# Block attention and gated MLP on one core: the order of all instructions set by a list scheduler in the kernel

## The chip, the core and the metric

One core of a Trainium2 chip. It has five engines that run at the same time, each in the order of its own queue: TensorE (matmul, PE in the rows; its weight loads are PEld), VectorE (DVE), ScalarE (ACT), GpSimd (POOL) and SyncE (SP), which here only starts DMA transfers. They wait for each other through semaphores. The metric is the device time of the one core in microseconds (us), the median of several runs.

## The reference

Eight images (batch) of 576 tokens with 8 heads of 64. Attention works only inside chunks of 64 tokens; its output, laid side by side over the heads, is the input of a gated MLP whose gate mixes tokens:

```python
scores = scale * np.matmul(q_c, k_c.transpose(0, 1, 2, 4, 3))     # 64x64 blocks
attn = np.exp(scores - max); attn = attn / (sum + 1e-09)
x = np.matmul(attn, v_c)                                           # (8, 576, 512)
h = gelu_tanh(x @ w_in)                                            # 512 -> 1024
u, v = h[..., :512], h[..., 512:]
v_n = (v - mu) / np.sqrt(var + 1e-06) * g_ln
v_s = np.einsum('ts,bsd->btd', w_sg, v_n) + b_sg[None, :, None]
out = x + (u * v_s) @ w_out
```

## The kernel before

All is float32, and each big product is done as three products of a high and a low part (names ending in h and l). The tokens are cut into 36 tiles of 128 for the attention; a tile passes through `att_scores` (S: matmuls of line 380 or 411, then maximum, exponential and sum on VectorE and ScalarE, then the division), `att_transpose` (T: VectorE's 32x32 transpose of line 450 and copies of lines 453 to 460 on ScalarE and VectorE, which write `ptT`; the first five tiles are transposed on TensorE, line 441), and `att_out` (O: matmuls of line 478 or 498, then `keep` splits the result into `xh` and `xl`).

For each image there are then `v_unit` (five or four token tiles, 12 matmuls each, line 544; gelu into `hs`, statistics of lines 550 to 553, scaling of lines 559 to 568 into `v` or `z`), four `u_unit` (24 matmuls, line 581, gelu into `u2`), four `s_unit` (the token mixing, 28 matmuls, line 601; `gh` and `gl` are the split gate), and the output product: `o_unit` for images 0 and 1, `o_fast` for the others (seven block products, line 672). `w_sums` makes sums of blocks of `w_out` on GpSimd for `o_fast` (tiles `r`, tag `tmp`, lines 250 to 274), once, in image 2. The weights `w_in` come as 64-bit words and are split in `pair_begin` and `pair_end` (L, W, w for the v half, X, x for the u half), `w_out` in `o_w` (Y). `keep_clock` (D) runs matmuls on a constant whose result nobody reads.

The string `START` (line 44) is the order in which the code of images 0 and 1 calls these steps; the loop at line 771 does the rest, with the attention of the next image put into slots between the units by `SLOTS`. The tile layer below takes the code's order as a priority, keeps a model of its own, and orders every engine's queue from that. Buffers come from pools: the tag `tmp` has four (`hs`, `blocks`, `ot`, `r`, staging), PSUM `pm` has four, `u2`, `v`, `pt` and `ptT` one each.

Of the kernel before, what the change touches and what calls it, by code (L numbers as in the profile page):

```python
# [3 lines left out]

# [5 lines left out]

F32 = mybir.dt.float32
F32R = mybir.dt.float32r
# [65 lines left out]
G_BLOCK = {(0, 0): 0, (1, 0): 1, (1, 1): 2, (0, 1): 3}  # L78


def segments(t):
# [9 lines left out]

@with_exitstack
def block_attention_gated_mlp(ctx: ExitStack, tc: tile.TileContext, qkv, w_in, w_out, w_sg, g_ln, b_sg, out):
    nc = tc.nc
    const = ctx.enter_context(tc.tile_pool(name="const", bufs=1))
    att = ctx.enter_context(tc.tile_pool(name="att", bufs=2))
    xp = ctx.enter_context(tc.tile_pool(name="xp", bufs=2))
    mp = ctx.enter_context(tc.tile_pool(name="mp", bufs=1))
    tmp = ctx.enter_context(tc.tile_pool(name="tmp", bufs=4))
    small = ctx.enter_context(tc.tile_pool(name="small", bufs=3))  # L100
    ps_m = ctx.enter_context(tc.tile_pool(name="ps_m", bufs=4, space=PSUM))

    def split(hi, lo, src, hi_eng, lo_eng):
        if hi_eng is nc.scalar:
# [466 lines left out]

    u2 = {}

    def u_unit(b, dt):
        pm = ps_m.tile([P, 2, 512], F32, name="pm")
        dc = slice(dt * P, (dt + 1) * P)
        i = 0
        for kt in range(KT):
            for a, c in ((win_l, xh[b]), (win_h, xl[b]), (win_h, xh[b])):
                for j in range(2):  # L580
                    nc.tensor.matmul(  # L581
                        pm[:, j, :HS], a[:, kt, dc], c[:, kt, j * HS : (j + 1) * HS], start=(i == 0), stop=(i == 11)
                    )
                i += 1
        if dt == 0:
# [155 lines left out]
    def att_slots(b, n):  # L741
# [18 lines left out]
    def keep_clock(n):  # L760

        spare = ps_m.tile([P, 2, 512], F32, name="pm")
        for _ in range(n):
            nc.tensor.matmul(spare[:, 0, :P], ident, ident, start=True, stop=True)

    steps["D"] = keep_clock
    steps["G"], steps["g"] = lambda k: load_w_sg(), split_w_sg
    steps["Y"] = lambda k: o_w(k // 2, k % 2)
# [2 lines left out]
    for b in range(2, B):  # L771
# [3 lines left out]
        slots = att_slots(b, len(units))  # L775
        for i, ((f, k), after) in enumerate(zip(units, slots)):
# [5 lines left out]
            for g, tiles in after:  # L782
                g(*tiles)
    o_fast(B - 1, 3)


# [42 lines left out]
```

## Time and profile before

| | |
|---|---|
| median of 3 runs | 534.28 us (534.09 to 535.17) |
| the profiled execution | 533.52 us, of which the span of the trace is 531.7 |
| instructions in the trace | 12411 |
| mean granted clock of TensorE | 0.981 of 2.4 GHz |
| DMA | 46.58 MB, mean 88 GB/s |
| ScalarE table loads | 32, mean 1283 ns |

The page gives one execution. TensorE is the busiest engine, and what it waits for is the first thing to read; a stretch in which its clock is low costs time without any wait being shown. The engines that feed it (VectorE and ScalarE for the attention tiles) are read by what stands in their queues before the instruction that TensorE waits for.

### The profile page before, as it was taken

What the parts mean: (1) busy time and instruction counts of PE and PEld (TensorE: products, weight loads), DVE (VectorE), ACT (ScalarE), POOL (GpSimd) and SP (SyncE); (2) the same over time, 40 slices, a digit from 0 to 9 for tenths busy, and PEclk for the clock granted to TensorE, in tenths of its full rate; (3) what the DMA queues carried; (4) which work ended last, traced back from release to release, by engine and by line L of the source; (5) the groups of instructions that cost most, each with busy time, mean ns of one, the idle gap of its engine ahead of it and who ended that gap; (6) DMA issues with size and microseconds to landing.
All of it is one profiled execution on the core that took longest, in us unless ns stands there. A gap on an engine that the chain in (4) does not pass through costs nothing.

```text
span 531.7 us, 12411 instructions
## 1 busy us (share of the span) xinstructions
PE 499.4 (94%) x5202; PEld 460.9 (87%) x5206; DVE 381.2 (72%) x719; ACT 287.9 (54%) x493; POOL 85.1 (16%) x83
## 2 busy tenths in 40 slices
PE   1999998899999979999999989999999979999996
PEld 1776888799999869998999879988999869998996
DVE  6895849986766787797658685797758685476156
ACT  5679557762433868537752477427752577313221
POOL 0032300030110257011300131011300131002000
PEclk9999998999999979999999999999999998999999
DMA  8765011212245522415120422414121400010002
GB/s 331 286 191 176 0 41 44 80 46 75 95 165 131 168 60 61 121 35 138 48 71 30 152 48 82 120 46 138 42 68 40 150 21 20 2 66 24 1 1 89
DMA packets 52683, 46.58 MB, mean 88 GB/s; under 512 B 35218, under 2 KB 45458, under 8 KB 52628
## 3 DMA queue, kind: packets, MB, share of 16 engines
q1 hardware_dynamic: 52628, 45.80, 27.8%
q8 instruction: 41, 0.67, 0.5%
q14 instruction: 14, 0.11, 0.1%
HBM read 36.34 MB, written 9.44 MB: 86 GB/s over the span
## 4 chain that ended last, share of the span: by engine, by line
PE 44%; DVE 10%; ACT 6%; POOL 2%; issue 1%; DVEq 0%; POOLq 0%; ACTq 0%
PE pm L601 12%; PE pm L581 11%; PE pm L672 11%; PE pm L544 7%; PE pm L478 2%; DVE gl L108 1%; POOL sm L553 1%; DVE sm L550 1%; DVE pt L387 1%; DVE nmax L384 1%; DVE v L562 1%; DVE xl L523 1%; ACT L391 1%; ACT xh L520 1%; DVE u L626 1%
## 5 line engine op out<-in xcount | busy, mean ns | idle before, releaser
L601 PE MATMUL pm<-wsg,v 128*128 128x288 f32 x768 | 109.5, 299 | 0.0
L601 PEld LDWEIGHTS pm<-wsg,v 128*128 128x128 f32 x768 | 105.4, 191 | 0.4
L553 POOL TENSOR_TENSOR sm<-sm,neg_half 128x1 f32<-128x1 f32 x36 | 36.5, 1015 | 235.2 <-DVE sm L552 235.2
L581 PE MATMUL pm<-xh,win_l 128*128 128x288 f32 x256 | 58.3, 310 | 0.3 <-ACT win_l L190 0.3
L581 PE MATMUL pm<-xh,win_h 128*128 128x288 f32 x256 | 56.5, 303 | 0.0
L581 PE MATMUL pm<-xl,win_h 128*128 128x288 f32 x256 | 56.5, 303 | 0.0
L544 PE MATMUL pm<-win_h,xl 128*128 128x512 f32 x128 | 51.5, 402 | 0.0
L105 ACT CAST gh<-u 128x576 fp32r<-128x576 f32 x32 | 21.5, 673 | 54.7 <-DVE u L605 43.7
L544 PE MATMUL pm<-win_l,xh 128*128 128x512 f32 x128 | 50.7, 396 | 0.0
L544 PE MATMUL pm<-win_h,xh 128*128 128x512 f32 x128 | 50.6, 395 | 0.0
L398 POOL TENSOR_TENSOR pt<-pt,nmax 128x512 f32<-128x512 f32 x27 | 28.7, 1082 | 133.0 <-DVE nmax L395 133.0
L605 DVE TENSOR_TENSOR u<-pm,u 128x576 f32<-128x576 f32 x32 | 23.9, 748 | 32.7 <-PE pm L601 32.5
L581 PEld LDWEIGHTS pm<-xh,win_l 128*128 128x128 f32 x256 | 43.1, 196 | 2.3 <-ACT win_l L190 0.7
L581 PEld LDWEIGHTS pm<-xl,win_h 128*128 128x128 f32 x256 | 42.7, 196 | 0.0
L581 PEld LDWEIGHTS pm<-xh,win_h 128*128 128x128 f32 x256 | 42.5, 195 | 0.0
L561 ACT ACTIVATE v<-hs,sm 128x512 fp32r<-128x512 f32 x32 | 23.1, 723 | 28.5 <-POOL sm L553 28.2
L550 DVE BATCH_NORM_STATS2 sm<-hs 128x6 f32<-128x512 f32 x36 | 24.4, 687 | 17.1 <-ACT hs L547 17.1
L478 PE MATMUL pm<-ptT,av 64*64 64x64 f32 x928 | 22.9, 232 | 11.1 <-ACT ptT L458 5.3
L478 PEld LDWEIGHTS pm<-ptT,av 64*64 64x64 f32 x928 | 18.9, 142 | 16.3 <-ACT ptT L458 9.0
L562 DVE SCALAR_TENSOR_TENSOR v<-hs,sm,v 128x512 fp32r<-128x512 f32 x32 | 24.1, 755 | 12.2 <-ACT v L561 11.8
L453 ACT COPY ptT<-blocks 128x512 f32<-128x512 f32 x31 | 19.0, 620 | 24.6 <-DVE blocks L450 17.2
L108 DVE TENSOR_TENSOR gl<-u,gh 128x576 fp32r<-128x576 f32 x32 | 25.0, 782 | 8.5 <-ACT gh L105 8.4
(163 smaller groups left out, 1062.6 us busy)
## 6 DMA issues: line engine op xcount, KB each, us to landing
qk<-qkv SPq DMA_DIRECT2D x31, 512.0 KB, 4.4
out_dram<-ot SPq DMA_DIRECT2D x31, 288.0 KB, 2.2
av<-qkv SPq DMA_DIRECT2D x116, 64.0 KB, 2.7
wsg<-w_in SPq DMA_DIRECT2D x4, 512.0 KB, 4.4
wout<-w_in SPq DMA_DIRECT2D x4, 512.0 KB, 7.8
st<-w_out SPq DMA_DIRECT2D x8, 256.0 KB, 3.1
qkv_w<-qkv SPq DMA_DIRECT2D x2, 768.0 KB, 10.6
stage<-w_sg SPq DMA_DIRECT2D x5, 288.0 KB, 4.2
```

The source lines that it names most:

```text
L108: lo_eng.tensor_tensor(lo, src, hi.bitcast(F32), op=ALU.subtract)
L398: eng.tensor_tensor(pt[:, i], pt[:, i], den[:, i].unsqueeze(2).broadcast_to([P, H, D]), op=ALU.mult)
L478: nc.tensor.matmul(pm[o, c, i, h // 2, :], vt[r, place, :], ptT[r, place].rearrange("p a s -> p (a s)"), start=True, stop=True,)
L544: nc.tensor.matmul(pv, a[:, kt, tok], c[:, kt, DH:], start=(i == 0), stop=(i == 11))
L550: nc.vector.bn_stats(st, h)
L553: nc.gpsimd.tensor_tensor(rs, rs, neg_half, op=ALU.pow)
L561: nc.scalar.mul(hi, h, rs)
L562: nc.vector.scalar_tensor_tensor(lo, h, rs, hi.bitcast(F32), op0=ALU.mult, op1=ALU.subtract)
L581: nc.tensor.matmul(pm[:, j, :HS], a[:, kt, dc], c[:, kt, j * HS : (j + 1) * HS], start=(i == 0), stop=(i == 11))
L601: nc.tensor.matmul(pm[:, j, :HS], a[:, dc], c[:, m, j * HS : (j + 1) * HS], start=(i == 0), stop=(i == len(ops) - 1))
L605: nc.vector.tensor_tensor(row, pm[:, :, :HS], row, op=ALU.mult)
L672: nc.tensor.matmul(pm[:, e, :HS], a[:, k, e * P : (e + 1) * P], c[:, k, :], start=(first and i == 0), stop=(i == len(ops) - 1), skip_group ...
```

## The change

Every call on an engine is only recorded (`Recorder`, `Plan.add`): its operands, the buffers it uses and, by the cells of memory that it reads and writes, which earlier calls it must follow. Each gets a price from its shape (`Op.price`). After the last call, `emit` runs a list scheduler three times (`run`): every engine takes, among the calls whose inputs are there, the one with the earliest due time among those that can start within 200 ns of the first; TensorE takes the one that can start first among its next 96 matmuls; a buffer of a pool can be taken when its last user is done. Due times (`due`) go back from TensorE's order of the run before. The calls are then issued in the order of their planned starts, with the tile layer told to keep that order. Which instructions there are, and how many on each engine, stays the same.

```diff
-v01 A8 B8 O4 x0 X1 v02 x1 X2 v03 X3 v04 u00 x2 g0 g1 u01 x3 g2 g3 u02 P5 g4 u03 T5 s00 T6 P7 s01 Q5 s02 T7 T8
+v01 A8 B8 O4 x0 X1 v02 x1 X2 v03 X3 v04 U0 x2 g0 g1 U1 x3 g2 g3 g4 F0 u02 F1 P5 u03 T5 s00 T6 P7 s01 Q5 s02 T7 T8
...
+AHEAD = 96
+WAIT = {"tensor": 100, "gpsimd": 120}
...
+        if self.engine == "sync":
+            size = self.ins[0].size() * 4
+            return (460 if self.ins[0].ap[-1][1] >= P else 640), 2000 + size / 400
+        if self.engine == "vector":
+            one = len(self.ins) == 1 and not psum and self.method in ("tensor_copy", "tensor_scalar")
+            return 75 + (0.53 if one else 1.04) * n, 80
+        if self.engine == "scalar":
+            return 100 + 0.82 * n + (100 if len(self.outs) > 1 else 0), 100
+        return (850 if "pow" in str(self.kwargs.get("op")) else 200 + 1.8 * n), 42
...
+        at = None
+        for _ in range(3):
+            at = self.run(users, after, at)
+        engines = {getattr(self.nc, e).engine for e in ENGINES}
+        with tc.manual_schedule(engines=engines):
+            for k in sorted(range(len(ops)), key=lambda k: (at[k], k)):
+                op = ops[k]
+                getattr(getattr(self.nc, op.engine), op.method)(*op.args, **op.kwargs)
...
+                    ks = [k for k in tensor[pe : pe + AHEAD] if start[k] is None]
...
+                t0 = min(found)[0]
+                if e == "tensor":
+                    t, k = min(found)
...
+                t, k = min(
+                    (late[k] + (1300 if ops[k].table not in (0, table) else 0), b, k) for b, k in found if b <= t0 + 200
+                )[1:]
...
-    nc = tc.nc
-    const = ctx.enter_context(tc.tile_pool(name="const", bufs=1))
...
+    nc = Plan(tc.nc)
...
-    make_identity(nc, eye)
+    nc.gpsimd.memset(eye, 0.0)
+    nc.gpsimd.affine_select(
+        out=eye, in_=eye, compare_op=ALU.not_equal, fill=1.0, base=0, pattern=[[-1, P]], channel_multiplier=1
+    )
...
+        if later:
+            held[dt] = pm
+        else:
+            u_act(dt, pm)
...
+    nc.emit(tc)
```

`U0` and `F0` part a `u_unit` of image 0 into its matmuls and its gelu. In the changed kernel every row carries line 224, since all calls are issued there; the names of the tiles tell them apart.

SyncE at the start of the program, before (`wsg`, `wout` receive the v half of `w_in`, `qk`, `qkv` and `av` the attention inputs of tiles 0 to 4):

```order
L214 DMA wsg_0_105<-w_in 128x1024
L346 DMA qk_107<-qkv 128x1024
L355 DMA av_109<-qkv 128x512
L346 DMA qk_111<-qkv 128x1024
L355 DMA av_113<-qkv 128x512
L214 DMA wsg_1_115<-w_in 128x1024
L214 DMA wout_0_148<-w_in 128x1024
L342 DMA qkv_w_167<-qkv 128x1536
L342 DMA qkv_u_175<-qkv 128x1536
L214 DMA wout_1_183<-w_in 128x1024
```

The same place now:

```order
L224 DMA qk_92<-qkv 128x1024
L224 DMA wsg_0_91<-w_in 128x1024
L224 DMA qkv_w_101<-qkv 128x1536
L224 DMA qk_94<-qkv 128x1024
L224 DMA wsg_1_96<-w_in 128x1024
L224 DMA av_93<-qkv 128x512
L224 DMA wout_0_99<-w_in 128x1024
L224 DMA wout_1_103<-w_in 128x1024
L224 DMA av_95<-qkv 128x512
L224 DMA qkv_u_102<-qkv 128x1536
```

The first tile's `qk` is now ahead of the weights, and the last quarter of the v half (`wout_1`) moves from tenth place to eighth.

GpSimd, before, from image 2's attention stage on (`r` are the sums for `o_fast`, `sm` the powers that `v_unit` waits for, `pt` the divisions of attention tiles):

```order
L398 TENSOR_TENSOR pt_2164<-pt_2164,nmax_2162 128x512 x2
L553 TENSOR_TENSOR sm_2215<-sm_2215,neg_half_90 128x1
L553 TENSOR_TENSOR sm_2238<-sm_2238,neg_half_90 128x1
L250 TENSOR_TENSOR r_2317<-wout_0_1192,wout_1_1193 128x512
L250 TENSOR_TENSOR r_2319<-wout_0_1192,wout_1_1193 128x512
L553 TENSOR_TENSOR sm_2269<-sm_2269,neg_half_90 128x1
```

Now the sums stand between image 1's four powers (`sm_189` to `sm_203`) and image 2's first (`sm_276`):

```order
L224 TENSOR_TENSOR sm_189<-sm_189,neg_half_83 128x1
L224 TENSOR_TENSOR r_307<-wout_0_194,wout_1_195 128x512
L224 TENSOR_TENSOR sm_193<-sm_193,neg_half_83 128x1
L224 TENSOR_TENSOR sm_199<-sm_199,neg_half_83 128x1
L224 TENSOR_TENSOR sm_203<-sm_203,neg_half_83 128x1
L224 TENSOR_TENSOR r_308<-wout_0_194,wout_1_195 128x512
L224 TENSOR_TENSOR r_309<-r_307,r_308 128x512
L224 TENSOR_TENSOR r_319<-wout_0_194,wout_1_195 128x512
L224 TENSOR_TENSOR r_308<-r_308,r_319 128x512
L224 TENSOR_TENSOR pt_225<-pt_225,nmax_224 128x512 x2
L224 TENSOR_TENSOR r_307<-r_308,r_307 128x512
L224 TENSOR_TENSOR pt_237<-pt_237,nmax_236 128x512 x2
```

Six of the eight operations of the sums are among these rows; the other two follow soon after, and all eight are now ahead of image 2's first power.

VectorE, before, in image 4's attention stage, between the two transposes of one pair of tiles (`blocks_3697` and `blocks_3731`):

```order
L559 SCALAR_TENSOR_TENSOR hs_3686<-hs_3686,sm_3688,g_bc_89 128x512
L562 SCALAR_TENSOR_TENSOR v_3527<-hs_3663,sm_3665,v_3527 128x512
L460 COPY ptT_3696<-blocks_3697 32x8x32
L550 BN_STATS sm_3719<-hs_3717 128x6
L562 SCALAR_TENSOR_TENSOR v_3527<-hs_3686,sm_3688,v_3527 128x512
L551 BN_AGGR sm_3719<-sm_3719 128x2
L450 STREAM_TRANSPOSE blocks_3731<-pt_3614 128x512
L552 TENSOR_SCALAR sm_3719<-sm_3719 128x1
L559 SCALAR_TENSOR_TENSOR hs_3717<-hs_3717,sm_3719,g_bc_89 128x512
L460 COPY ptT_3696<-blocks_3731 32x8x32 x2
```

The same pair now (`blocks_432` and `blocks_436`):

```order
L224 SCALAR_TENSOR_TENSOR hs_426<-hs_426,sm_427,g_bc_82 128x512
L224 STREAM_TRANSPOSE blocks_432<-pt_419 128x512
L224 SCALAR_TENSOR_TENSOR v_410<-hs_423,sm_424,v_410 128x512
L224 SCALAR_TENSOR_TENSOR v_410<-hs_426,sm_427,v_410 128x512
L224 STREAM_TRANSPOSE blocks_436<-pt_419 128x512
L224 COPY ptT_431<-blocks_432 32x8x32 x2
L224 BN_STATS sm_430<-hs_429 128x6
L224 COPY ptT_431<-blocks_436 32x8x32 x2
```

Two instructions now stand between the transposes; before there were thirteen.

ScalarE behind it, before:

```order
L588 ACTIVATE u2_3763<-pm_3738 128x576
L453 COPY ptT_3696<-blocks_3731 128x512
L458 COPY ptT_3696<-blocks_3731 32x8x32
L566 ACTIVATE z1_0_91<-hs_3717,sm_3719 64x512
L566 ACTIVATE z1_1_92<-hs_3717,sm_3719 64x512
L567 CAST z2_0_93<-z1_0_91 64x512
L567 CAST z2_1_94<-z1_1_92 64x512
L458 COPY ptT_3696<-blocks_3731 32x8x32
```

And now:

```order
L224 COPY ptT_431<-blocks_432 128x512
L224 COPY ptT_431<-blocks_432 32x8x32 x2
L224 ACTIVATE hs_434<-pm_433 128x512
L224 COPY ptT_431<-blocks_436 128x512
L224 COPY ptT_431<-blocks_436 32x8x32 x2
L224 ACTIVATE u2_438<-pm_437 128x576
```

The last copy of the second tile no longer stands behind four operations on `z`, and the gelu of `u2` follows the copies.

## Rows read from the trace of the kernel before

**Rows 1.** The page, section 1: busy time, share of the span, instructions

```profile
PE 499.4 (94%) x5202; PEld 460.9 (87%) x5206; DVE 381.2 (72%) x719; ACT 287.9 (54%) x493; POOL 85.1 (16%) x83
```

**Rows 2.** Stretches: start:end, length, each engine's busy time (instructions), clock, DMA

```profile
0.00:36.90 36.90, 23.60 (x341) 18.49 (x343) 28.92 (x63) 23.26 (x67) 4.38 (x9) 1.00 0.78 272
36.90:75.90 39.00, 37.66 (x309) 30.33 (x309) 24.59 (x48) 25.78 (x59) 9.67 (x8) 1.00 0.31 92
75.90:99.10 23.20, 20.25 (x245) 19.20 (x243) 21.42 (x44) 17.30 (x28) 0.00 (x0) 0.93 0.14 36
...
180.00:200.00 20.00, 16.80 (x176) 14.52 (x178) 16.77 (x33) 13.91 (x22) 10.30 (x10) 0.85 0.31 94
200.00:217.00 17.00, 16.52 (x253) 15.86 (x250) 11.79 (x20) 12.75 (x19) 9.14 (x7) 0.98 0.21 56
...
240.00:360.00 120.00, 116.92 (x1274) 109.46 (x1273) 88.41 (x159) 68.89 (x103) 18.46 (x18) 0.99 0.28 82
360.00:480.00 120.00, 117.20 (x1215) 110.42 (x1215) 82.21 (x149) 64.19 (x96) 15.89 (x16) 0.97 0.20 59
```

**Rows 3.** The same columns, three 10 us pieces

```profile
310.00:320.00 10.00, 7.40 (x148) 6.52 (x149) 9.20 (x19) 7.32 (x13) 2.87 (x3) 0.84 0.30 79
430.00:440.00 10.00, 7.21 (x150) 6.26 (x149) 9.23 (x18) 6.86 (x13) 2.13 (x3) 0.81 0.12 28
440.00:450.00 10.00, 10.00 (x66) 10.00 (x66) 5.57 (x12) 8.79 (x12) 2.05 (x2) 0.85 0.12 27
```

**Rows 4.** What TensorE waited for: us in total, times, longest

```profile
PE pm L478 <- ACT ptT L458: 6.9, 6, 2.2
PE banks L441 <- DVE first_pts L431: 6.0, 2, 5.5
PE pm L411 <- DMA qk<-qkv: 5.7, 1, 5.7
```

**Rows 5.** Timeline of TensorE, start of the program: start us, us, what [idle before]

```profile
35.92 0.66 PE L441 MATMUL banks<-ident,first_pts 128*128 128x128 f32 x4 [0.34 <-ACT xf L517]
...
36.88 0.50 PE L544 MATMUL pm<-win_h,xl 128*128 128x512 f32 x1
```

**Rows 6.** VectorE alone, busy in one stretch on tile wsg

```profile
26.30:36.90 10.60, 7.12 (x10) 1.00 0.63 182
```

**Rows 7.** Timeline of ScalarE, image 0's attention stage

```profile
75.51 0.43 ACT L151 ACTIVATE st<-st 128x256 f32<-128x256 uint32 x1 [3.24 <-DMA st<-w_out]
```

**Rows 8.** Timeline of GpSimd beside image 2's third attention pair

```profile
192.19 3.04 POOL L250 TENSOR_TENSOR r<-wout,wout 128x512 f32<-128x512 f32 x2 [1.84 <-DVE v L562]
```

**Rows 9.** VectorE, image 4's attention stage

```profile
308.57 0.69 DVE L450 STREAM_TRANSPOSE blocks<-pt 128x512 f32<-128x512 f32 x1
...
314.29 0.68 DVE L450 STREAM_TRANSPOSE blocks<-pt 128x512 f32<-128x512 f32 x1
```

**Rows 10.** ScalarE, the same stretch

```profile
316.10 1.46 ACT L566 ACTIVATE z<-hs,sm 64x512 fp32r<-64x512 f32 x2
...
318.85 0.40 ACT L458 COPY ptT<-blocks 32x256 f32<-32x256 f32 x1
```

**Rows 11.** TensorE, the same stretch

```profile
316.11 0.27 PE L478 MATMUL pm<-ptT,av 64*64 64x64 f32 x1 [2.18 <-ACT ptT L458]
```

**Rows 12.** VectorE beside a GpSimd instruction, and without

```profile
29.00 1.77 DVE L144 SCALAR_TENSOR_TENSOR wsg<-wsg 128x512 int32<-128x512 int32 x1
...
30.77 0.68 DVE L144 SCALAR_TENSOR_TENSOR wsg<-wsg 128x512 int32<-128x512 int32 x1
```

**Rows 13.** GpSimd in that time

```profile
28.95 1.28 POOL L108 TENSOR_TENSOR xl<-xf,xh 128x512 fp32r<-128x512 f32 x1 [3.51 <-ACT xh L105]
```

**Rows 14.** The chain that ended last, one token tile of image 4

```profile
292.03 2.81 PE pm L544 x12
...
294.92 0.61 ACT hs L547
...
298.50 0.75 DVE v L562
```

More of the change, by code (lines that the diff above doesn't have):

```diff
@@ L3 @@
 from contextlib import ExitStack
+import numpy as np
 import concourse.bass as bass
@@ L7 @@
 from concourse import mybir
-from concourse.masks import make_identity
 from concourse._compat import with_exitstack
@@ L78, with is_ap, cells @@
 G_BLOCK = {(0, 0): 0, (1, 0): 1, (1, 1): 2, (0, 1): 3}
+ENGINES = ("tensor", "vector", "scalar", "gpsimd", "sync")
+AHEAD = 96
+WAIT = {"tensor": 100, "gpsimd": 120}
+TABLES = {AF.Exp: 1, AF.Gelu_apprx_tanh: 2}
+def is_ap(a):
+    return hasattr(a, "rearrange") and hasattr(a, "tensor")
+def cells(a):
+    width = mybir.dt.size(a.dtype)
+    (step, n), *free = a.ap
+    row, at = a.offset // step, a.offset % step
+    idx = np.array([at])
+    for st, c in free:
+        idx = (idx[:, None] + st * np.arange(c)[None, :]).ravel()
+    psum = a.space == PSUM
+    unit = 2048 if psum else 128 if step * width > 256 else 4
+    mask = 0
+    for i in np.unique(idx * width // unit):
+        mask |= 1 << int(i)
+    if psum:
+        return (mask, 0, 0, 0)
+    return tuple(mask if row < 32 * (q + 1) and row + n > 32 * q else 0 for q in range(4))
@@ new lines, in meet, with within, __init__, price @@
+def meet(a, b):
+    return any(x & y for x, y in zip(a, b))
+def within(a, b):
+    return all(x & ~y == 0 for x, y in zip(a, b))
+class Op:
+    def __init__(self, engine, method, args, kwargs):
+        self.engine, self.method, self.args, self.kwargs = engine, method, args, kwargs
+        outs = [kwargs["out"] if "out" in kwargs else args[0]]
+        ins = [a for a in (*args[("out" not in kwargs):], *kwargs.values()) if is_ap(a)]
+        ins = [a for a in ins if a is not kwargs.get("out") and a is not kwargs.get("accum_out")]
+        self.outs, self.ins = outs + [a for a in [kwargs.get("accum_out")] if a is not None], ins
+        self.deps, self.succ, self.tiles = set(), [], []
+        self.table = next((TABLES.get(f, 0) for f in (*args, *kwargs.values()) if isinstance(f, AF)), 0) if engine == "scalar" else 0
+        self.cost, self.lag = self.price()
+    def price(self):
+        n = max(a.free_size() for a in self.outs[:1] + self.ins[:2])
+        psum = any(a.space == PSUM for a in self.outs + self.ins)
+        if self.engine == "tensor":
+            x = self.ins[-1]
+            n = self.outs[0].free_size()
+            if x.dtype == F32R:
+                return 4.6 + 0.447 * n, 160
+            if x.dtype == BF16:
+                return 4.6 + 0.42 * n, 160
+            if self.ins[0].ap[0][1] == D:
+                return 39, 160
+            return (115 if self.method == "transpose" else 1.76 * n + 10), 160
+        if self.engine == "sync":
[7 more added lines that the diff above has]
+        return (850 if "pow" in str(self.kwargs.get("op")) else 200 + 1.8 * n), 42
@@ L93, in block_attention_gated_mlp, with pool @@
 def block_attention_gated_mlp(ctx: ExitStack, tc: tile.TileContext, qkv, w_in, w_out, w_sg, g_ln, b_sg, out):
-    nc = tc.nc
-    const = ctx.enter_context(tc.tile_pool(name="const", bufs=1))
[L96 to L101, printed above, removed]
+    nc = Plan(tc.nc)
+    def pool(name, bufs, **kwargs):
+        return nc.pool(ctx.enter_context(tc.tile_pool(name=name, bufs=bufs, **kwargs)), bufs)
+    const = pool("const", 1)
+    att = pool("att", 2)
+    xp = pool("xp", 2)
+    mp = pool("mp", 1)
+    tmp = pool("tmp", 4)
+    small = pool("small", 3)
+    ps_m = pool("ps_m", 4, space=PSUM)
     def split(hi, lo, src, hi_eng, lo_eng):
@@ L572, in block_attention_gated_mlp, with u_unit @@
     u2 = {}
-    def u_unit(b, dt):
+    def u_unit(b, dt, later=False):
         pm = ps_m.tile([P, 2, 512], F32, name="pm")
@@ L584, in u_unit, with u_act @@
                 i += 1
+        if later:
+            held[dt] = pm
+        else:
+            u_act(dt, pm)
+    held = {}
+    def u_act(dt, pm=None):
+        pm = held.pop(dt) if pm is None else pm
         if dt == 0:
@@ L764, in keep_clock @@
             nc.tensor.matmul(spare[:, 0, :P], ident, ident, start=True, stop=True)
+    steps["U"] = lambda k: u_unit(0, k, later=True)
+    steps["F"] = u_act
     steps["D"] = keep_clock
```

145 lines of the change are left out of this document (added).

## The prediction

> **What bounds the kernel now.** First the busy times: TensorE works 499.4 of 531.7 us [rows 1], so it idles 32.3 us, and no order of the other engines can give back more than that, with one exception: the clock. The profile's mean granted clock is 0.981, which over 531.7 us is 10.1 us at the difference between full speed and nothing, or about 20 us at the lower of the two levels, 1.2 instead of 2.4 GHz.
>
> Second, where the idle time lies, by stretches [rows 2]; idle is length less the first busy time. The start to the first matmul of `v_unit` (36.88 us, [rows 5]) has 13.3 us, the rest of image 0's v and u units 1.3 us, the stage after it (75.9 to 99.1) 2.95 us at a clock of 0.93. The stretch 180 to 217 has 3.2 and 0.5 us at 0.85 and 0.98. Of the 3.1 us in 240 to 360, 2.6 lie in one piece, 310 to 320, at 0.84, and of the 2.8 us in 360 to 480 all lie in 430 to 440, at 0.81, with 0.85 in the piece behind it [rows 3]. So there are five places, and at each of the last four the clock falls right behind the gap: the gap is paid for twice.
>
> Third, for whom TensorE waits [rows 4]: behind the start, `att_out` (line 478) waits for `ptT`, the transposed probabilities, which ScalarE's line 458 copies last, 6.9 us in 6 waits. At the start it is 5.7 us for the first DMA and 6.0 us for a softmax. TensorE's work itself is not at issue: the change takes no matmul away.
>
> Fourth, what stands in the way of those copies. In image 4's stage the two transposes of a pair of tiles are 5.7 us apart on VectorE, at 308.57 and 314.29 [rows 9]; the copy of the second stands behind four operations on `z`, 316.10 to 318.85, on ScalarE [rows 10], and TensorE stood idle for 2.18 us up to 316.11 [rows 11]. Image 6 repeats it. In image 2's stage GpSimd adds two sums of 3.04 us together just there [rows 8]. So these gaps are made by the order of queues, not by the amount of work: VectorE is busy 72% and ScalarE 54% of the span [rows 1].
>
> **The change part by part.** The instructions are the same, so each part is a move. Sums are against the profiled execution, 533.52 us (1.8 more than its span); the median of the runs stands 0.8 us above it.
>
> TensorE's own order hardly moves behind the start: units and attention steps follow each other nearly as before. The gain there must come from the suppliers being earlier.
>
> *Start.* What the first `v_unit` needs last is the split of the fourth quarter of `w_in`, whose load moves from tenth to eighth place, while the split of the u half, which it does not need, moves behind it. VectorE, the fullest engine there, worked 28.92 us up to 36.9 [rows 2], of which 7.1 us on `wsg` from 26.3 on were for the u half [rows 6]. That leaves at most 21.8 us, or 22.6 with the 0.8 us before its first operation. At the share of busy time that it had (28.92 of 36.9, 78%) the `v_unit` would start at 27.8. Bounds: 22.6 and 36.9; I take 28, by the second figure, since ScalarE's share was lower. Behind it stand now one tile's transposes and one more `att_out`: 0.66 us [rows 5], and about 1.1 us by the matmuls of such a tile (an estimate from the same stage), 1.7 together. Gain 8.9 - 1.7 = 7.2 us, between 12.6 and 0. The first DMA's 5.7 us stays, but for the 1 us or so that `qk` gains by going first.
>
> *75.9 to 99.1.* Price of the place: 2.95 us idle and 0.07 x 23.2 = 1.6 us of clock, 4.6 together. Changed: image 1's first matmuls of `v_unit` may go ahead of an `att_out` that is not ready, and the divisions and transposes of a pair stand closer. Not changed: ScalarE waits 3.24 us for `st`, a load of `w_out` whose buffer comes free only by the scores [rows 7], and that wait still stands ahead of the exponential. I take 3.5, bounds 0 and 4.6.
>
> *Image 2's stage.* 3.2 + 0.5 us idle, and 0.15 x 20 + 0.02 x 17 = 3.3 us of clock: 7.0. The sums leave the place altogether, and the copies move forward. I take 6, bounds 2 (gaps go, clock stays) and 7.
>
> *Image 4's stage.* 2.6 + 0.16 x 10 = 4.2 us; two instructions between the transposes where thirteen stood, and no `z` ahead of the last copy. Is the pair then in time? The first transpose ran at 308.57 [rows 9]; with its 0.69 us and two instructions of 0.75 us [rows 14] the second ends at 311.5, and its copies, 0.40 us each for the two small ones [rows 10] and about a transpose's time for the large one, end at 313. TensorE came for it at 316.11 - 2.18 = 313.9 [rows 11]. It is close: I take 3.5, bounds 1 and 4.2.
>
> *Image 6's stage.* 2.8 us, 0.19 x 10 and 0.15 x 10 of clock: 6.2. The same argument; I take 5, bounds 1.5 and 6.2.
>
> *New stalls.* An order worked out from prices holds only as far as these hold, and every engine now keeps it whatever happens. Nothing of this is in the trace of before. By its nearest rows one stall is 2.2 us [rows 11] and up to 3.4 us of clock. From 0 (none) to 10 (two of the worst); I take 3, nearer to none, as the two orders are alike on TensorE.
>
> One behaviour speaks against the change. VectorE's operation of line 144 took 1.77 us while GpSimd ran a 1.28 us addition, and 0.68 us without it [rows 12, 13]. No price in the planner knows this. The Trainium skill, "GPSIMD Engine Reference", section 1 (Specifications), says the SBUF interfaces of GpSimd are shared with VectorE, and that instructions with two SBUF inputs contend; the rows agree. By it the eight moved sums would each lengthen a VectorE operation in their new place, between the splits of `w_out`. They did so in their old place as well, where VectorE could not afford it, and image 1's units are none of the five places: by the row the move costs at most 8 x 1.1 us of VectorE's slack, which I price at nothing.
>
> Sum: -7.2 - 3.5 - 6 - 3.5 - 5 + 3 = -22.2, so 533.5 - 22.2 = 511.3 for a profiled run and 512 for the median.
>
> **The rivals.**
>
> *The start does not move.* For it: DMA is busy 0.78 of the start [rows 2], and the fifth tile's inputs are still eleventh in the queue. Against: TensorE waited 5.7 us for its first DMA and afterwards for VectorE and ScalarE [rows 4]. Then the start gives 0: 519. Chance 0.17.
>
> *All gaps close.* The four places give their whole prices (22.0 instead of 18), no new stall comes, and the start gives 10 since VectorE is fuller than 78%: 534.3 - 32 = 502. For it: nothing but order stands in the way in [rows 9, 10]. Against: the second tile of image 4's pair has under 1 us of slack. Chance 0.17.
>
> *The gaps move.* Half of the four places' gain (9) and the start's 7.2 come, but 8 us of new stalls with them, since real waits differ from the planned ones: 534.3 - 8 = 526. For it: the contention above and the wait for `st` are outside the prices. Chance 0.13.
>
> *Slower: the sums hold `tmp`.* Two of the four `tmp` buffers hold sums from image 1's units to image 2's, some 60 us, in which eight `ot`, five `blocks` and five `hs` need one each. A `hs` is held from 294.92 to 299.25, 4.3 us, and a `v_unit` takes 2.81 us [rows 14]. With two buffers free that is 2.2 us a unit, and nothing waits; with one, as when an `ot` waits for its store, 1.5 us a unit. If all 18 pay that, 27 us, and the clock falls once (3.4): 512 + 30 = 542. It decides from 1.25 us on each of the 18. Against: nothing says they come all at the worst moment. Chance 0.07.
>
> **How the numbers follow.** The forecast has 0.46. Its own bounds with the start between 22.6 and 32 give 500 to 522. The range holds rivals one and three and most of the second: 499 to 529, with 0.2 outside (the last rival, and the ends of the second and third). A difference of 0.2%, 1.1 us, is what a measurement can tell from none. Only the last rival is slower, 0.07; no change needs the gains to cancel within 1 us, 0.02; faster 0.91.
>
> **What would show it.** The first matmul of `v_unit` near 28 us; no `att_out` wait over 1 us in images 2, 4 and 6, and a mean clock of 0.99 or more; TensorE idle near 17 us, with busy near 490; `r` done before image 2's v units. The forecast is wrong if the first `v_unit` still starts behind 34 us, if the waits of TensorE name other lines than before with the same sum, or if `hs` or `ot` wait for buffers between 110 and 180 us.

## The result, and the profile after

The changed kernel took 513.54 us, the median of four runs (512.99 to 515.15), against 534.18 of the kernel before (533.82 to 535.17). The ratio is 0.9616, with a 95% interval from 0.9591 to 0.9641. The forecast was 512. All of it lies inside the profiled span, which fell from 531.7 to 511.2 us.

The busy times, to be set beside [rows 1]:

```profile
PE 493.0 (96%) x5201; PEld 453.9 (89%) x5206; DVE 390.7 (76%) x719; ACT 288.8 (57%) x493; POOL 80.8 (16%) x83
```

TensorE idles 18.2 us instead of 32.3, and is busy 6.4 us less for the same matmuls, at a mean granted clock of 0.997 instead of 0.981. The forecast had asked for an idle time near 17, a busy time near 490 and a clock of 0.99 or more.

Part of the smaller idle time is no gain. Before, TensorE stood idle for 5.70 us until its first scores began. Now it runs 16 matmuls of `keep_clock`, whose result nobody reads, in that time, and the first scores begin at 6.08 us:

```profile
2.37 3.78 PE L224 MATMUL pm<-ident 128*128 128x128 f32 x16 [2.37 <-ACT ident L224]
6.08 0.79 PE L224 MATMUL pm<-qk 64*64 64x64 f32 x32
```

The stretches of the changed kernel, with the columns of [rows 2] (start:end, length, each engine's busy time, clock, DMA share, GB/s). The first three are cut at the same units as there: the start, image 0's v and u units, and the stage behind them. Then come the new gap, image 2's v and u units, and, in the last two rows, images 4 to 7:

```profile
0.00:28.40 28.40, 22.31 (x303) 16.69 (x306) 22.14 (x46) 19.26 (x60) 4.24 (x9) 1.00 0.99 337
28.40:68.40 40.00, 39.33 (x354) 31.63 (x345) 34.06 (x65) 29.48 (x65) 7.72 (x8) 1.00 0.37 100
68.40:86.20 17.80, 17.76 (x242) 17.16 (x241) 16.37 (x33) 14.20 (x21) 0.00 (x0) 1.00 0.15 35
...
150.00:166.30 16.30, 12.45 (x157) 11.51 (x157) 10.41 (x19) 8.85 (x16) 1.05 (x1) 0.90 0.52 153
166.30:198.90 32.60, 31.30 (x383) 27.76 (x382) 26.90 (x51) 26.02 (x40) 9.10 (x9) 1.00 0.36 102
...
281.50:400.00 118.50, 117.90 (x1290) 110.69 (x1289) 89.72 (x160) 68.59 (x102) 17.94 (x18) 1.00 0.30 86
400.00:505.00 105.00, 104.78 (x961) 99.45 (x960) 69.79 (x121) 45.39 (x70) 12.60 (x13) 1.00 0.12 36
```

Idle is again length less the first busy time. Images 4 to 7 are almost without gaps, at full clock. Behind the start one stretch has much idle time and a lower clock together, 150 to 166.3: 3.85 us at 0.90. It is none of the five places of before.

The longest waits of TensorE (us in total, times, longest), to be set beside [rows 4]:

```profile
PE pm L224 <- issue: 3.0, 2, 2.7
PE pm L224 <- ACT ptT L224: 2.4, 3, 1.3
PE pm L224 <- ACT ident L224: 2.4, 1, 2.4
PE pm L224 <- DVE wout L224: 1.2, 1, 1.2
PE pm L224 <- DVE xl L224: 1.2, 1, 1.2
```

`ptT` fell from 6.9 us to 2.4; the 6.0 us for `first_pts` and the 5.7 us for the first load are gone from the top, the latter because `keep_clock` fills them.

A ledger shows where the time went: the start of the first matmul of a unit in both traces, and how far the changed kernel is ahead. A term is the change of that lead between two units. Leads and terms are worked out from the starts before rounding, so the last digit can differ by one.

| up to the first matmul of | before, us | after, us | lead | term measured | term forecast |
|---|---|---|---|---|---|
| image 0's s units (the start) | 75.90 | 68.40 | 7.50 | +7.5 | 7.2 |
| image 1's u units (75.9 to 99.1) | 111.73 | 100.87 | 10.87 | +3.4 | 3.5 |
| image 2's v units (new stall) | 171.59 | 166.32 | 5.27 | -5.6 | -3 |
| image 3's v units (image 2's stage) | 237.81 | 227.48 | 10.32 | +5.05 | 6 |
| image 5's v units (image 4's stage) | 357.03 | 342.21 | 14.81 | +4.5 | 3.5 |
| image 7's v units (image 6's stage) | 475.82 | 455.24 | 20.57 | +5.8 | 5 |

The sum is 20.6 us against 22.2 forecast, and behind image 7's v units the lead does not change any more.

### The profile page after: what moved, and what is told of

It is laid out like the page before. It is cut to its first block, busy times and chain, and to the rows that moved or that the text cites. A ratio compares the mean times of both kernels' runs of the same rounds, so it can differ in the third digit from the quotient of the medians.

```text
span 511.2 us, 12425 instructions
## 1 busy us (share of the span) xinstructions
PE 493.0 (96%) x5201; PEld 453.9 (89%) x5206; DVE 390.7 (76%) x719; ACT 288.8 (57%) x493; POOL 80.8 (16%) x83
## 4 chain that ended last, share of the span: by engine, by line
PE 56%; DVE 24%; ACT 11%; issue 3%; DMA 2%; POOL 1%; SPq 1%; DVEq 0%; POOLq 0%; ACTq 0%
PE pm L224 55%; DVE nmax L224 5%; ACT ptT L224 3%; DVE sm L224 2%; DVE pt L224 2%; DVE st L224 2%; DVE blocks L224 2%; DVE hs L224 2%; ACT L224 2%; ACT z L224 2%; DVE v L224 1%; ACT xf L224 1%; PE banks L224 1%; ACT pt L224 1%; DVE gl L224 1%
## 5 line engine op out<-in xcount | busy, mean ns | idle before, releaser
L224 PEld LDWEIGHTS pm<-wsg,v 128*128 128x128 f32 x768 | 103.9, 188 | 0.9 <-issue 0.5
L224 ACT COPY ptT<-blocks 32x256 f32<-32x256 f32 (+1 forms) x93 | 44.2, 476 | 34.2 <-DVE blocks L224 32.0
L224 POOL TENSOR_TENSOR sm<-sm,neg_half 128x1 f32<-128x1 f32 x36 | 31.0, 863 | 197.7 <-DVE sm L224 193.5
L224 PE MATMUL pm<-xh,win_l 128*128 128x288 f32 x256 | 55.6, 299 | 0.0
L224 PE MATMUL pm<-gh,wout 128*128 128x288 f32 x272 | 54.0, 300 | 0.0
L224 PEld LDWEIGHTS pm<-gh,wout 128*128 128x128 f32 x272 | 43.3, 192 | 0.3
L224 PEld LDWEIGHTS pm<-xh,win_l 128*128 128x128 f32 x256 | 41.4, 188 | 1.3
L224 PEld LDWEIGHTS pm<-xl,win_h 128*128 128x128 f32 x256 | 41.1, 188 | 0.0
L224 ACT ACTIVATE hs<-pm 128x512 f32<-128x512 f32 x36 | 21.3, 596 | 27.1 <-PE pm L224 23.0
L224 PE MATMUL pm<-gl,wout 128*128 128x288 f32 x136 | 35.8, 300 | 0.0
```

Of the source, the lines that this page charges most:

```text
L224: getattr(getattr(self.nc, op.engine), op.method)(*op.args, **op.kwargs)
```

## The experiments

Medians, and ratios to the kernel before, which ran on the same chip beside each. The runs were taken in groups, on more than one chip, so the ratio compares them better than the median:

| run | median, us | ratio, 95% interval |
|---|---|---|
| the changed kernel again | 512.73 | 0.9608 (0.9577 to 0.9640) |
| late pair | 536.46 | 1.0058 (1.0025 to 1.0091) |
| start's order | 523.04 | 0.9764 (0.9703 to 0.9824) |
| start's loads alone | 519.06 | 0.9733 (0.9705 to 0.9761) |
| start's loads, rest planned | 513.74 | 0.9603 (0.9564 to 0.9642) |
| TensorE in program order | 514.15 | 0.9639 (0.9604 to 0.9673) |
| sums late | 512.18 | 0.9570 (0.9512 to 0.9629) |
| stores first | 513.94 | 0.9600 (0.9546 to 0.9654) |
| sums between | 510.93 | 0.9581 (0.9554 to 0.9608) |
| five buffers | 508.78 | 0.9523 (0.9489 to 0.9556) |
| sums earlier | 508.13 | 0.9503 (0.9475 to 0.9531) |

The changed kernel again: 

> The changed kernel again, as the reference for this group. Every theory expects 512.5 to 515.5, with the first v unit between 28 and 30.5 us, by what the runs so far showed of the start.

It came as expected, 512.73, with the first v unit at 28.80 us.

Most experiments plan as the changed kernel does, then fix the queues of some engines and move instructions in them. The hook is the same each time, and only `moved` differs:

```diff
         for _ in range(3):
             at = self.run(users, after, at)
+        at = self.run(users, after, at, self.moved(at))
```

### Is it the order in the pair's queues?

The run "late pair" moves these instructions back:

```diff
+    def moved(self, at):
+        q = self.queues(at)
+        for b, dve, copies in self.late:
...
+            for e, ks in (("vector", [lo, aggr, dve[0], aggr + 1, aggr + 3, *dve[1:]]), ("scalar", [mul, u, *copies[:-1], *z, copies[-1]])):
+                i = q[e].index(aggr if e == "vector" else copies[0])
...
```

> The changed kernel with one thing undone, in images 2, 4 and 6 alone: VectorE's second transpose of the attention pair stands behind the layer-norm statistics of the fifth v unit again, and ScalarE's last ptT copy behind both z2 casts, as in rows 9 and 10; TensorE's, GpSimd's and SyncE's orders are those of the changed kernel. Theory (the order of the two queues makes the gap before att_out, and the gap costs a second time in the granted clock behind it): a wait for ptT of about 2 us comes back in each of the three images (2.18 in row group 11), the clock of the stretch behind it falls to half for 1.5 to 3 us, and the time rises by 3 to 5 us an image, to 522.5 to 528.5. Rival 1 (the gap costs itself and nothing more): 3 x 2.2 = 6.6 us, so 518.5 to 521.5 with the clock unchanged. Rival 2 (the gap went for another reason, the pair's order does nothing): 513.5 within 1.5.

Measured: 536.46, slower than any of the three. The whole gain of the change was lost by moving a handful of instructions in three images. TensorE in image 4's stage (timeline, with the idle time before a group in brackets), and two 10 us pieces with the columns of [rows 3]:

```profile
311.55 0.69 PE L226 MATMUL pm<-ptT,av 64*64 64x64 f32 x32
315.56 0.47 PE L226 MATMUL pm<-ptT,av 64*64 64x64 f32 x2 [3.31 <-ACT ptT L226]
318.76 1.02 PE L226 MATMUL pm<-ptT,av 64*64 64x64 f32 x27 [2.74 <-ACT ptT L226]
```

```profile
310.00:320.00 10.00, 3.95 (x92) 3.46 (x93) 4.99 (x12) 5.40 (x10) 1.84 (x2) 0.73 0.09 20
320.00:330.00 10.00, 10.00 (x112) 9.88 (x108) 5.69 (x8) 5.37 (x6) 0.00 (x0) 0.76 0.51 139
```

The gap is 6.05 us, not the 2.2 that I took from [rows 11]: TensorE waits once for the second tile's large copy and once for its last small one. That the order of the two queues makes a gap, and that the gap costs more than itself, is shown. The three images lose 8.6, 8.55 and 8.4 us between one image's units and the next's. Of 8.55 in image 4, 6.05 are the gap, and 2.5 more are lost behind it, where TensorE was busy for all of 320 to 330 us at a granted clock of 0.76. So the gap is paid for 1.4 times, which is the theory against rival 1. (The trace is of an execution of 539.29 us.)

The size is not that of the gap before, since this run is not the old order in full. VectorE's two transposes are further apart than the 5.72 us of [rows 9]:

```profile
306.65 0.71 DVE L226 STREAM_TRANSPOSE blocks<-pt 128x512 f32<-128x512 f32 x1
...
313.74 0.68 DVE L226 STREAM_TRANSPOSE blocks<-pt 128x512 f32<-128x512 f32 x1
```

And TensorE's order is the changed kernel's, with the matmuls of both tiles one behind the other. In the kernel before, TensorE did the next tile's scores and six matmuls of a `u_unit` ahead of the second tile's last 30 matmuls, and so waited only 0.23 us for its last copy:

```profile
317.26 0.85 PE L581 MATMUL pm<-xh,win_l 128*128 128x288 f32 x2
...
319.31 1.08 PE L478 MATMUL pm<-ptT,av 64*64 64x64 f32 x30 [0.23 <-ACT ptT L458]
```

The changed order thus depends more on its suppliers than the old one did.

### What sets the start?

First ("start's order"), VectorE and ScalarE in the old order up to the first v unit, with the new loads:

```diff
+    def moved(self, at):
+        q = self.queues(at)
+        del q["tensor"]
+        for e, start in (("vector", VECTOR_START), ("scalar", SCALAR_START)):
+            ks = [int(k) for k in start.split()]
+            q[e] = ks + [k for k in q[e] if k not in ks]
...
```

> The changed kernel with the order of VectorE and ScalarE up to the first v unit put back to that of the kernel before, instruction by instruction; the loads keep the changed kernel's order, TensorE's order is free in this stretch alone. Theory of the prediction (the vector and scalar queues set the start): the first v unit, at 28.46 us in the changed kernel and at 36.88 before, goes back to 33 to 37, and the time to 518 to 522. Rival (the loads' order and their earlier start set it): the first v unit stays under 30.5 and the time under 515.5.

The first `v_unit` matmul went back to 36.95 us, against 36.88 before [rows 5], and 9.8 us of lead were lost by the end; 523.04 is 1 us over the range. The edit leaves TensorE to the planner for the whole program, and not in the start alone. VectorE's work on `wsg`, which holds a part of the v half and then of the u half, up to the first `v_unit`, 12.40 us in the kernel before, is 5.74 us in the changed kernel and 11.19 in this run:

```profile
0.00:28.40 28.40, 5.74 (x11) 1.00 0.99 337
0.00:36.90 36.90, 11.19 (x18) 0.91 0.82 279
```

Then the loads alone ("start's loads alone"), with the other four queues fixed:

```diff
+        loads = sorted(q["sync"])[:11]
+        q["sync"] = loads + [k for k in q["sync"] if k not in loads]
```

> The changed kernel, with SyncE's first eleven loads put back to the order of the kernel before (the first quarter of w_in ahead of the first qk, the fourth quarter tenth again); the other four queues keep the changed kernel's order. Theory (the queues of VectorE and ScalarE carry the start; putting them back cost 8.5 us up to the first v unit in the run before this): the first v unit moves by 2 us at most from 28.5 us, and the time stays within 513 to 516. Rival (the loads' order matters as much): the first v unit at 32 us or later, 517 to 521.

Here my theory failed: the first `v_unit` came at 34.71 us and the time was 519.06. Its trace names the wait:

```profile
PE pm L225 <- DMA qkv_w<-qkv: 5.9, 1, 5.9
```

TensorE's queue holds the scores of a tile that the old order loads five places later, and everything behind them waits. So there was one more run ("start's loads, rest planned"), with the old loads and the other queues planned around them:

```diff
+        return {"sync": loads + [k for k in q["sync"] if k not in loads]}
```

> The changed kernel, with SyncE's first eleven loads in the order of the kernel before, and the other four queues put in order by the planner around these loads. Theory 1 (it is the agreement of the queues: the 6.3 us that the same loads cost under the changed kernel's other orders were a wait of TensorE for qkv_w, which the old order of loads brings late): the first v unit at 28 to 30.5 us, 512.5 to 515.5. Theory 2 (the loads' order itself sets the start, since the fourth quarter of w_in comes two places later): the first v unit at 32 us or later, 516.5 to 520.

The first `v_unit` came at 29.10 us and the time was 513.74: theory 1. The order of loads is therefore not what brought the first `v_unit` forward; with other queues that fit it, the old one does nearly as well. It did lose 2.7 us of the start's 7.5 up to image 0's s units, and had 1.7 of them back by image 2's. Left is the order of VectorE and ScalarE. The run with their old order also had old queues beside new loads, and TensorE waited 2.0 us for `qkv_w` in it, a wait that the kernel before does not have, so a part of its 8.5 us may be mismatch; it ended at the old start nevertheless. The two queues were not put back one at a time.

### What closed the gap ahead of image 1's v units?

The run "TensorE in program order":

```diff
+        q = self.queues(at)["tensor"]
+        n = q.index(313)
+        return {"tensor": q[:n] + sorted(q[n:])}
```

> The changed kernel, with TensorE's matmuls from the first v unit on in the order in which the program notes them; the other queues are put in order by the planner around that. TensorE's order differs in five places alone: four pieces of the attention and weight work in image 0's v units, one of image 1's att_out behind its first v matmuls, one of image 1's output, one of image 2's pair. Theory of the prediction (the gain is in the suppliers' queues, TensorE's order hardly moves): 513 to 516, with 0 to 3 us lost in image 0's units and in the stage before image 1's v units. Rival (TensorE's order carries the gain of 3.4 us in that stage and more): 517 to 522.

The time was within the theory's range, 514.15, but the gain of this place hangs on TensorE's order. TensorE in program order comes to image 1's first `v_unit` matmul at 91.17 us instead of 86.23, 4.9 later, and 1.3 come back up to the u units: 3.6, all that the place had gained. The rows of that run:

```profile
87.66 1.11 PE L225 MATMUL pm<-ptT,qkv_w 64*64 64x64 f32 x32 [1.31 <-ACT ptT L225]
89.69 1.55 PE L225 MATMUL pm<-ptT,qkv_w 64*64 64x64 f32 x32 [0.92 <-ACT ptT L225]
91.17 0.79 PE L225 MATMUL pm<-win_h,xl 128*128 128x512 f32 x1
```

In the changed kernel the v unit begins ahead of these `att_out` and goes on between them, and TensorE waits once, for 0.84 us:

```profile
87.70 0.32 PE L224 MATMUL pm<-ptT,qkv_w 64*64 64x64 f32 x2 [0.84 <-ACT ptT L224]
```

The run won 2.5 us of it back behind, 1.7 of them in the new stall.

### What is the new stall?

The rows of the changed kernel. TensorE; then VectorE, with what it waited for; then SyncE's queue:

```profile
153.72 0.69 PE L224 MATMUL pm<-qk 64*64 64x64 f32 x32 [1.17 <-DVE xl L224]
159.02 0.30 PE L224 MATMUL pm<-ptT,av 64*64 64x64 f32 x2 [2.69 <-issue]
```

```profile
148.60 0.71 DVE L224 STREAM_TRANSPOSE blocks<-pt 128x512 f32<-128x512 f32 x1 [2.08 <-DMA out_dram<-ot]
154.62 0.71 DVE L224 STREAM_TRANSPOSE blocks<-pt 128x512 f32<-128x512 f32 x1 [0.38 <-DMA out_dram<-ot]
157.85 0.76 DVE L224 TENSOR_TENSOR ot<-pm,xf 128x576 f32<-128x576 f32 x1 [2.52 <-DMA out_dram<-ot]
158.64 0.60 DVE L224 COPY ptT<-blocks 32x256 f32<-32x256 f32 x2
```

```profile
146.16 5.82 SPq L224 DMA_DIRECT2D av<-qkv  x8
152.08 2.52 SPq L224 DMA_DIRECT2D out_dram<-ot  x2
...
157.91 0.60 SPq L224 DMA_DIRECT2D av<-qkv  x1
```

Each of the three waiting instructions of VectorE needs a buffer in which an `ot` stands until its store has landed; the copies for `att_out` are queued behind it. By the program's addresses, two of the four `tmp` buffers hold sums over this time, and `ot` and `blocks` take turns in the other two. The store issued at 152.08 is of an `ot` that was complete at 146.5; eight loads of `av`, 0.6 us each and more, stood ahead of it. So two things could be at work: the sums hold buffers (theory A), or the stores come late out of SyncE's queue (rival B). "issue" in TensorE's row is where the profile shows no releaser.

Sums held back until image 2's v units:

```diff
+        if op.engine == "gpsimd" and op.outs[0].tensor.name.split("_")[0] == "r":
+            op.deps.add(self.hold)
...
+            if b == FAST and i == 4:
+                nc.hold = len(nc.ops) - 1
```

> The changed kernel, with GpSimd's sums r held back until image 2's five v units are done (they stand about where the kernel before had them); everything is ordered by the same planner. Theory A (two of the four tmp buffers held by the sums cause the new 5.6 us between image 1's output and image 2's first v unit): the lead of the first v unit of image 2 over the kernel before rises from 5.3 to 9.5 to 11 us, and image 2's attention stage loses most of the 4.6 us it had won, because the sums run beside it again: 511 to 514. Rival B (the stores of ot stand in SyncE's queue behind eight loads of av): the lead of image 2's first v unit stays at 5 to 7 us, and with the loss in the attention stage the time is 515.5 to 518.

Image 2's first `v_unit` came 6.6 us earlier than in the changed kernel, 11.8 us ahead of the kernel before where 9.5 to 11 were expected, and in the stretch of the stall TensorE is busy 9.89 of 10 us. Then 4.7 us are lost in image 2's attention stage, of which 0.7 come back by image 3's v units:

```profile
150.00:160.00 10.00, 9.89 (x157) 9.48 (x156) 7.63 (x14) 4.36 (x8) 1.04 (x1) 1.00 0.70 204
...
190.00:200.00 10.00, 6.62 (x50) 6.28 (x48) 9.44 (x10) 5.99 (x10) 9.65 (x7) 1.00 0.00 1
200.00:210.00 10.00, 9.70 (x170) 9.44 (x171) 7.95 (x13) 6.87 (x9) 0.05 (x1) 0.83 0.46 112
```

GpSimd is busy 9.65 of 10 us there, as the sums stand ahead of the pair's divisions. So both halves of theory A held, the first with more than its size, and the time, 512.18, is in its range.

Stores first on SyncE:

```diff
+                if op.engine == "sync" and op.outs[0].tensor.name == "out_dram":
+                    late[k] = -1e6
```

> The changed kernel, with all engines' orders as they are but SyncE's: a store of the output goes first whenever it is ready by the planner's times, so one store of image 1 stands ahead of the eight loads of av it stood behind, and the second two loads further forward. Rival B of the new stall (SyncE's queue): the 5.6 us between image 1's output and image 2's first v unit shrink to 3 or less, 510 to 511.5. Theory A (the buffers held by the sums): it shrinks by under 1 us, 512.5 to 514.

No gain: 513.94, and the stall grew by 1.4 us. But this says little against rival B: with the stores moved, the buffers were handed out in another turn, and an `ot` got the buffer of the `ot` just before it. Its wait for that store was 3.7 us.

One more buffer, the order unchanged:

```diff
-    tmp = pool("tmp", 4)
+    tmp = nc.pool(ctx.enter_context(tc.tile_pool(name="tmp", bufs=5)), 4, 5)
```

> The changed kernel in its own order, with five tmp buffers on the chip where the planner still counts four. To make room it multiplies by a quarter of w_in instead of the layer-norm gains g_bc (whose load is left out) and uses one of the two low-word factors twice, so its output is not the reference's; its instructions are those of the changed kernel, up to that load. Theory A (the new 5.6 us between image 1's output and image 2's first v unit are a wait for a tmp buffer): the lead of image 2's first v unit over the changed kernel rises by 4 to 6 us, 507 to 510. Rival (the planned order itself stalls there: VectorE's queue, the loads of av, the splits of the sums): under 1.5 us, 512 to 514.

The median, 508.78, is in theory A's range, but the trace (of an execution of 510.49 us) has only 1.2 us more lead in that place, which is the rival's figure. Another 0.8 us of lead it has from ahead of that place, where the missing load of the gains may count. The waits of `blocks` are gone, and one of `ot` is longer:

```profile
155.89 0.76 DVE L224 TENSOR_TENSOR ot<-pm,xf 128x576 f32<-128x576 f32 x1 [3.86 <-DMA out_dram<-ot]
```

This `ot` takes the buffer of one whose store stood behind the eight loads. So rival B has a part too: it sets how long a buffer is away. How much of the 5.6 us is the one and how much the other stays open. That the stall goes when the sums are elsewhere, with the loads of `av` ahead of the stores as ever, is shown by sums late and by the two runs that follow.

Sums between the two places:

```diff
+        if step == "o13":
+            nc.hold = max(k for k, op in enumerate(nc.ops) if op.engine == "tensor")
+    for step in range(4):
+        w_sums(step)
     for b in range(2, B):
```

> The changed kernel, with GpSimd's sums r noted down before image 2's units instead of among them, and held back until the last matmul of image 1's output: they should stand between image 1's output and image 2's attention pair, in neither of the two places that wait. Theory A (the sums held tmp too long in the changed kernel, and ran beside the attention pair in the version that held them till image 2's v units were done): the lead of image 2's first v unit over the changed kernel rises by 5 to 6.5 us, as with the sums held late, and image 2's attention stage gives none of it back: 507 to 509.5. Rival (GpSimd's sums slow VectorE wherever they stand): half of it comes back as waits in image 2's v units and attention, 510 to 513.

The lead of image 2's first `v_unit` rose by 6.1 us, as expected, but 2.4 of it were lost by image 3's v units, 1.8 of them ahead of image 2's s units: 510.93, in the rival's range. VectorE just ahead of the pair, in that run:

```profile
168.21 1.20 DVE L224 TENSOR_TENSOR wout<-r,wout 128x512 fp32r<-128x512 f32 x1
169.34 1.78 DVE L224 TENSOR_TENSOR wx<-r,wx 128x512 fp32r<-128x512 f32 x1
171.05 0.68 DVE L224 TENSOR_TENSOR wx<-r,wx 128x512 fp32r<-128x512 f32 x1
```

GpSimd's sums ran beside the first two, the last of them up to 170.58, and not beside the third:

```profile
168.95 1.63 POOL L224 TENSOR_TENSOR r<-r 128x512 f32<-128x512 f32 x1
```

1.20 and 1.78 us against 0.68 is the lengthening of [rows 12], at another place. The changed kernel has it too, where image 1's units have no gap: 1.78 us at 128.66 beside a sum, 0.69 at 142.10 without one. How much of the 2.4 us is due to it was not tried.

Sums two output units earlier (the mark is `o11` instead of `o13`):

> As the version with the sums between, but the sums may begin two output units of image 1 earlier, so that they are over before image 2's attention pair comes to VectorE. Theory A (the tmp buffers; and in the version with the sums between, splits of the sums took 1.2 us on VectorE beside GpSimd, against 0.7, just ahead of the pair): the attention stage's 1.8 us come back, but the sums now hold buffers while four ot need theirs, so 1 to 5 us are lost before image 2's first v unit: 509.5 to 513.5. Rival (only the length of time that sums are held counts, not the place): no loss before the v unit, 507 to 509.

508.13, the lowest median (the interval of five buffers overlaps it), and the rival's result: the lead of image 2's first `v_unit` over the changed kernel rose by 6.3 us, nothing is lost there though the sums run among the last `ot`, and 1.9 us are still lost behind it, where an `ot` waits for a buffer again:

```profile
162.33 0.76 DVE L224 TENSOR_TENSOR ot<-pm,xf 128x576 f32<-128x576 f32 x1 [2.57 <-DMA out_dram<-ot]
```

Its interval, 0.9475 to 0.9531, lies below both that of the changed kernel (0.9591 to 0.9641) and that of its second measurement (0.9577 to 0.9640). That fits the length of time for which sums are held. In the changed kernel GpSimd has six of eight operations done by 137 us, and two sums stay in their buffers until image 1's output is over. For one of them the reason is in the program: its last split overwrites a weight block which that output still reads, and ScalarE waits for TensorE there up to 164.93. The other is needed by an operation that itself starts only at 167.17, as a buffer comes free. Here GpSimd's first sum starts at 149.33 us, some 10 us before that output is over.

## Why the prediction was right

The terms below mostly hold one by one, but that their sum came within 2 us is in part luck: the new stalls and image 2 came out 3.5 us worse than forecast, and images 4 and 6 and the start 2 us better.

*Start: 7.2 forecast, 7.5 measured; 28 us forecast for the first `v_unit`, 28.46 measured.* In the changed kernel VectorE worked 22.14 of 28.40 us, 78%, the share that the step kept.

```profile
28.46 0.50 PE L224 MATMUL pm<-win_h,xl 128*128 128x512 f32 x1
```

The step said that a load moves from tenth to eighth place and that the u half's split moves behind. The runs bear out the second, as a part of the order of VectorE and ScalarE (5.74 us on `wsg` ahead of the first `v_unit` where there were 12.40), and not the first: the old order of loads with planned queues starts at 29.1. The split was not moved alone.

*75.9 to 99.1: 3.5 forecast, 3.4 measured.* The step named two causes. The run with TensorE in program order loses all of the gain, so the first, the `v_unit` going ahead of `att_out`, is needed; whether it would do without the second was not tried. The general sentence ahead of the steps, that TensorE's order hardly moves behind the start and the gain must come from the suppliers, was wrong for this place. It was not right for images 4 and 6 either, where TensorE's order moved as well (under the late pair). As the step said, ScalarE's wait for `st` [rows 7] stayed; the changed kernel has it at

```profile
68.13 0.77 ACT L224 ACTIVATE st<-st 128x256 f32<-128x256 f32 x2 [3.36 <-DMA st<-w_out]
```

*Images 4 and 6: 3.5 and 5 forecast, 4.5 and 5.8 measured.* The rows of VectorE, ScalarE and TensorE that answer to [rows 9 to 11]:

```profile
297.28 0.70 DVE L224 STREAM_TRANSPOSE blocks<-pt 128x512 f32<-128x512 f32 x1
...
299.92 0.70 DVE L224 STREAM_TRANSPOSE blocks<-pt 128x512 f32<-128x512 f32 x1
```

```profile
300.71 1.48 ACT L224 COPY ptT<-blocks 128x512 f32<-128x512 f32 x3
```

```profile
302.18 1.17 PE L224 MATMUL pm<-ptT,av 64*64 64x64 f32 x62
```

The transposes are 2.64 us apart instead of 5.72, the last copy ends at 302.19, just as TensorE comes for the pair, and 62 matmuls run without a wait. Image 4's term is 0.3 above its upper bound: between the two units of the ledger TensorE's idle time fell by 2.5 us, as priced, and its busy time by 2.0, where 1.6 were priced as clock. Image 6's, 5.8 of 6.2, is nearly the whole price. That the order of the two queues can make or close the gap is shown by the late pair.

One reading of the step was wrong. It put the 2.18 us of [rows 11] down to the four operations on `z` too. That wait ends at 316.11, while those operations begin only at 316.10 [rows 10], so it was for the second tile's earlier copies, behind the late transpose. The copy that did stand behind `z` cost TensorE 0.23 us. The operations on `z` cost more only in the late pair, 2.74 us in its TensorE order.

*Image 2: 6 forecast, 5.05 measured.* The sums left the place, as forecast; where they were put back (sums late), 4.7 us were lost again, about 4 of them for good. A wait of 1.3 us for `ptT` remains, so the sign "no `att_out` wait over 1 us" was missed, and so was "`r` done before image 2's v units": two of the sums ran at 167 to 170 us.

*New stalls: -3 forecast, -5.6 measured.* This is the term that was mis-sized, within its bounds (0 to 10). It is one place, and the mechanism is that of the slower rival, with the sums in two of four buffers. That rival asked for 18 waits; there were three, of 5.0 us together on VectorE. What it left out is in SyncE's rows: a store that stands behind loads keeps its buffer away for longer than the `ot` itself needs. One of the prediction's own signs of being wrong came true here: an `ot` waits for a buffer at 157.85 us, between 110 and 180. The place stayed within the term's bounds all the same.

*The contention, priced at nothing.* In its new place it cost nothing that shows as a term. VectorE's busy time rose from 381.2 to 390.7 us for the same 719 instructions, but that is not the sums' place: with the sums late it is 392.2. Added up one by one, the durations grew from 413.0 to 417.1 us only; the rest is that they overlap less. In the sums between, the contention stood just ahead of the pair. The Trainium skill, "GPSIMD Engine Reference", section 1 (Specifications), has GpSimd and VectorE share their SBUF interfaces and contend when VectorE's instruction has two SBUF inputs; the trace agrees with 1.78 us against 0.68.

The clock did as forecast. By 10 us pieces it fell once behind the start, after the stall: 0.83 in 160 to 170 us. In the traces of the sums between and the sums earlier, which have no stall there, it stays at 1.00 up to 500 us, with a mean of 0.998.

One sum of the prediction does not come out. It says that its own bounds, with the start between 22.6 and 32, give 500 to 522. The lower end follows. With the start at 32 and every other term at its worse bound, the upper end is 534.3 - (3.2 + 0 + 2 + 1 + 1.5) + 10, or 537.

## What to carry to other kernels

Where in-order queues feed an engine that is 94% busy, look at what stands ahead of the last small instruction that it waits for: in the late pair four small operations on `z` and a few statistics cost 8.4 to 8.6 us an image, and with them behind the copy TensorE did not wait. Look also at what the fed engine has in hand for such a wait: in the kernel before, scores and other matmuls stood between the two tiles, and a similar order of suppliers cost less. A planner that sees only durations and buffer counts can move idle-engine work to where it holds scarce buffers, as it did here; check for each buffer how long it is away, its store's place in the queue included. When one queue is put back alone to test it, the others wait for what it brings late, so let the rest be planned around it before drawing a conclusion.

## What was not expected

The order of the loads alone was worth little, and without the other queues less than nothing: the same eleven loads cost 6.3 us up to the first `v_unit` beside queues planned for other loads, and 0.6 us beside queues planned for them.

One extra `tmp` buffer moved the wait from `blocks` to `ot` (from 2.5 and 2.5 us to 3.9 in one piece) rather than removing it, and moving the stores forward changed which tile got which buffer. In both, the turn in which buffers are handed out mattered, and not their number alone.

Eight stores of `ot`, 288 KB each, issued between 125 and 172 us in the changed kernel, landed 2.1 to 4.4 us after their issue, 2.4 in the median; the slowest keeps a buffer two microseconds longer.
